# Four edits at the two ends of an attention and two-layer kernel: where the gate's exponential stands, zero products ahead of the first scores, the order of the first unit's row blocks, and a last evacuation in two halves

## The chip, the cores and the metric

The kernel runs on one core of a Trainium2 chip. The metric is device time in microseconds (us) of one launch. Three runs of the kernel before took 921.33, 922.25 and 922.31 us; the median is 922.25. A difference of 0.2% is 1.84 us.

## The reference

The reference is an attention layer with a memory path, followed by two gated feed-forward layers, all in float32.

```python
# attention: B, H, S, D = 4, 8, 576, 64
scores = (q @ k.T) / 8, masked above the diagonal
a = softmax(scores);  local = a @ v
q_p = phi(q)                      # phi(x) = (x if x > 0 else exp(x) - 1) + 1
mem_out = (q_p @ M_prev) / (q_p @ z_prev + 1e-6)
g = 1 / (1 + exp(-beta))          # one number per head, the gate
x = g * mem_out + (1 - g) * local # reshaped to 2304 tokens x 512
# layer 1: w_in 512 x 2048, w_out 2048 x 512
x = softplus(x @ w_in) @ w_out
# layer 2: w_a, w_b 512 x 1536, w_out 1536 x 512
out = ((x @ w_a) * (x @ w_b)) @ w_out
```

## The kernel before

The program is recorded as a list of steps, each with the tiles that it reads and writes. Afterwards `Plan.order` places the steps on the five engines with a model of its own: each step has a time and a lag (the time from its end until a reader may start), set in `weigh`. TensorE (PE) keeps the order in which its steps were recorded, first all of the attention, and of the later stages only what fits where the model sees it wait. On VectorE (DVE), ScalarE (ACT), GpSimd (POOL) and the DMA queue of SyncE (SP) the ready step with the longest chain behind it goes first, and a step that isn't ready in the model is passed by. So a change of one lag can reorder steps far away. The orders are fixed when the program is built; on the chip each engine takes its own list from the front and waits where an operand is missing.

**Attention.** There are 16 units, each of two heads of one batch. For a unit, `loads_k` and `loads_v` fetch the operands (tiles kr, qr, vr) and `prep_k` splits k and q into a high and a low part (kh, kl, qh, ql; line 343 is the subtraction), so that three products of fast float32 give full precision. `score` (line 517) forms row blocks of 128 queries: block 0 is 128 keys wide, block 1 256, block 2 384 and block 3 512, for two heads. DVE then takes each block's row minimum with the mask (line 527, tiles eTrue and eFalse, numbers in mn) and ACT its exponential (line 531). The last 64 queries of two units at a time are done by `tails` (line 668) and `score_tail` (line 538, tile eT). So units come in pairs: the tails stand with the even unit, after its successor's operands are there.

Per unit, `prep_v` and `prep_v2` form phi (ACT lines 498 and 499, DVE line 502, tiles ph and pos), `memory` multiplies it with M and z (line 555) and divides (tiles nm and mo). M has been multiplied by the gate: `gates` (lines 441 to 448) loads beta by a DMA of eight words per partition (tile bt, line 685), takes its exponential on ACT, and finishes on POOL and DVE; `load_m` (line 456) multiplies on POOL. `turn` (line 597, copies at 603 and 605) transposes the exponentials, `turn_tail` (lines 614 to 618) those of the tails, `send` (lines 570 to 576) passes the reciprocal row sums through DRAM by two stores, one of nine rows of 128 words and one of 64 words, and reads them back spread over the partitions (tile rb); `finish` (line 643) multiplies by them (tile xx) and stores. PSUM has eight banks. The scores take banks 2 and 3 (block 2), 0 and 1 (blocks 0 and 1) and 4 and 5 (block 3), the tails of a pair banks 0, 1 and 4, 5, and the transposes go round the same banks, so each of these waits for the engine that empties the bank before it.

While the attention runs, DVE, ACT and POOL also decode and split the first weights of layer 1 (lines 757 to 770, tiles raw and wf) in what time is left.

**Layers.** Each of the four products is done by seven products of half-size blocks in three passes (lines 875 and 1019). The last stage (`Wide.group`, line 1019) writes the output of a token group; the very last block is copied out of PSUM by one ACT instruction (line 1032) and stored by one DMA on SP's queue (line 1061).

Of the kernel before, what the change touches and what calls it, by code (L numbers as in the profile page):

```python
# [10 lines left out]
F32R = mybir.dt.float32r  # L11
U32 = mybir.dt.uint32
AF = mybir.ActivationFunctionType
# [9 lines left out]
HALF = 384  # L23
GT = 2 * HALF
NG = NT // GT
# [6 lines left out]
START, CONST, WORDS = 6272, 1280, 55680  # L32
SWITCH, LANES, AHEAD = 190, 6, 500
TAIL = 4
SEND, SENDC = 0, 5
RINGS = [2, 3, 0, 1, 4, 5], [4, 5, 2, 3, 0, 1]

# [18 lines left out]
class Plan:  # L56
# [103 lines left out]
    def weigh(self, s):  # L160

        kw, call = s.kw, s.call.__name__
        size = lambda ap: ap.free_size()
        o = kw["ap" if call == "memset" else "out"]
        inp = lambda ap: hasattr(ap, "tensor") and ap.tensor.name == self.psum
        s.size, s.mode, n = 0, None, size(o)
        two = call in ("tensor_tensor", "scalar_tensor_tensor", "tensor_tensor_reduce")
        s.port = s.eng == "POOL" or s.eng == "DVE" and not any(inp(v) for v in kw.values()) and n > 64
        if call == "dma_start":
            run = min(self.run(o), self.run(kw["in_"]))  # L170
            each = 14.5 + run / 4.85 if o.tensor.name in self.place else 33.3 + run / 8.7
            s.size = o.nbytes() / (4 * run) * each / 16
            s.time, s.lag = 420, 3000
        elif s.eng == "PE":
            s.lag = 205
            if call == "transpose" or kw.get("is_transpose"):
                s.time = n / 1.2 + 3
                s.mode = 128, 128, True
            else:
                plain = kw["rhs"].dtype != F32R  # L180
                rows, cols = (64 if x <= 64 else 128 for x in (kw["lhsT"].partition_size(), size(kw["lhsT"])))
                s.time = (1 + plain) * max(n / 1.2 + 3 if plain else n / 2.4 + 13.3, cols * 0.42 * (128 // rows))
                s.time /= 16384 / rows / cols
                s.mode = rows, cols, False, plain
        elif s.eng == "DVE":
            s.lag = 125
            s.time = n / (0.96 if two or any(inp(v) for v in kw.values()) else 1.92) + 68
            if hasattr(kw.get("scalar1"), "tensor"):
                s.time += 64
        elif s.eng == "ACT":  # L190
            s.lag = 50 if "accum_out" in kw else 145
            s.time = n * 0.834 + (50 if inp(kw["in_"]) else 94) + (184 if "accum_out" in kw else 0)
            if not isinstance(kw.get("scale", 1.0), float) or kw.get("scale") == REBIAS:
                s.time += 90
        else:
            s.lag = 90
            s.time = n * 2.1 + 210 if two else n * 0.82 + 200
# [126 lines left out]
def tile_kernel(ctx: ExitStack, tc: tile.TileContext, qt, kt, vt, mz, be, w_in, w_out, w_a, w_b, w_2, out):  # L324
    nc = tc.nc
    plan = Plan(tc)
    V, A, G, PE, SP = (
        Engine(plan, n, e) for n, e in (("DVE", nc.vector), ("ACT", nc.scalar), ("POOL", nc.gpsimd), ("PE", nc.tensor), ("SP", nc.sync))
    )

    def f(ap):
        return ap.bitcast(F32)
# [18 lines left out]
    bank = plan.track(nc.alloc_psum_tensor("bank", [128, 8, 512], F32).ap())  # L351
# [43 lines left out]
    RAW, WL, X0, X1, X2, SUMS = 0, 4096, 14848, 25600, 36352, 49664  # L395
# [3 lines left out]
    for n, words in (("kr", S), ("qr", 640), ("qh", 512), ("ql", 512), ("kh", S), ("kl", S), ("ph", 640)):  # L399
        at = [early(words), early(words)] + [more(words)] * (n in ("kr", "qr"))  # L400
# [23 lines left out]
        return bank[:, k : k + 2] if wide else bank[:, k]  # L424

    nc.scalar.preload_act_table_set("exp_and_others")
    G.memset(ap=ident, constant=0.0)
    G.affine_select(out=ident, in_=ident, compare_op=ALU.not_equal, fill=1.0, base=0, pattern=[[-1, 128]], channel_multiplier=1)
    G.memset(ap=mask1, constant=0.0)
# [2 lines left out]
    for j in range(2):  # L432
        G.affine_select(
            out=mask2[64 * j : 64 * j + 64, 1, 224:], in_=mask2[64 * j : 64 * j + 64, 1, 224:], compare_op=ALU.is_ge, fill=MASKED,
# [5 lines left out]
    def gates():  # L440
        A.activation(out=gt, in_=bt, func=AF.Exp, scale=-1.0)
        G.tensor_scalar(out=gt, in0=gt, scalar1=1.0, scalar2=1.0, op0=ALU.mult, op1=ALU.add)
        V.reciprocal(out=gt, in_=gt)
        pairs = gt.rearrange("p (n j) -> p n j", j=2)
        for odd in range(2):
            for j, r in enumerate(both):
                rnd(G, gp[r, odd::2], pairs[r, odd::2, j ^ odd])
        G.tensor_scalar(out=og, in0=gt, scalar1=-1.0, scalar2=1.0, op0=ALU.mult, op1=ALU.add)
# [4 lines left out]
    def load_m(b):  # L453
        m = mzs[b % 2]
        SP.dma_start(out=m, in_=mz[b])
        G.tensor_tensor(out=m[:, :, 0:64], in0=m[:, :, 0:64], in1=gp.unsqueeze(2).to_broadcast([128, NP, 64]), op=ALU.mult)
# [220 lines left out]
    def attention():  # L677
        nu = len(order)
        for name, part in (("eT", slice(S, 640)),):
            for t in where[name][0]:  # L680
                G.memset(ap=t[:, part], constant=0.0)
        for t in where["vr"][0]:
            G.memset(ap=t[low, 512:640], constant=0.0)
        order[0].loads_k()
        A.dma_start(out=bt, in_=be.partition_broadcast(128))
        order[1].loads_k()
        order[0].loads_v()
        order[0].prep_k(True)
        order[1].prep_k()
        order[0].prep_v()  # L690
        gates()
        load_m(0)
        at = lambda n: order[n] if 0 <= n < nu else None
        for n in range(nu + 2):
            cur, prev, old, nxt = (at(n - d) for d in (0, 1, 2, -1))
            if cur:
                if n % 2 == 0:
                    cur.begin()
                cur.score(2, 2)
                cur.score(0, 0, 1)  # L700
                cur.score(4, 3)
            if prev:
                prev.memory(2)
            if nxt and n:
                nxt.prep_k()
            if cur:
                cur.prep_v2()
            if n + 2 < nu:
                order[n + 2].loads_k()
            if cur and n:  # L710
                cur.loads_v()
            if nxt:
                if nxt.p == 0:
                    load_m(nxt.b)
                nxt.prep_v()
            if old:
                old.use()
                old.finish()
            if cur:
                if n % 2 == 0:  # L720
                    nxt.begin()
                    tails(((cur, 0), (nxt, TAIL)))
                cur.sums()
                cur.over()
            if prev:
                rings["psT"] = [RINGS[n % 2], 0]
                if n % 2:
                    prev.send(bank[0:10, SEND, 0:128])
                prev.turn(A, [(0, 0)])
                prev.turn(V, [(1, 0)])  # L730
                prev.turn(A, [(0, 1), (0, 3)])
                prev.turn(V, [(1, 1), (1, 3)])
                prev.turn(A, [(0, 2), (1, 2)])
                prev.turn_tail()
                prev.spread()
                if cur and n % 2:
                    cur.send(bank[0:10, SENDC, 0:128])

    attention()


# [214 lines left out]
    class Wide:  # L956
# [69 lines left out]
        def group(self, g):  # L1026


            def out(m):
                def out_(i, j, s, bank):  # L1030
                    if bank is not None:
                        A.activation(out=s, in_=bank, func=AF.Copy)
                    self.store(g, 2 * (2 - i) + m, j - 1, s)

                return out_

            units = [Seven(self.mult(m), out(m)) for m in range(2)]

            def piece(n, k):
                def go():  # L1040
                    if k == 0:
                        for u in units:
                            u.open(n)
                        if n in (5, 6, 7, 4):
                            self.sums(n)
                    x = self.parts(n, k)
                    for u in units:
                        u.mm(n, x, k)
                    if k == self.nu // 2 - 1:
                        for u in units:  # L1050
                            u.after(n)

                return go

            return [piece(n, k) for n in SEQ for k in range(self.nu // 2)]
# [1 line left out]
    def store_y(g, m, j, s):  # L1057
        SP.dma_start(out=ys[g][:, m, HALF * j : HALF * j + HALF], in_=s)

    def store_out(g, m, j, s):  # L1060
        SP.dma_start(out=out[128 * m : 128 * m + 128, GT * g + HALF * j : GT * g + HALF * j + HALF], in_=s)

    second = Wide(
        NU1, gs, wod,
# [177 lines left out]
```

## Time and profile before

| | |
|---|---|
| median of three runs | 922.25 us |
| span of the profiled execution, first to last instruction | 918.2 us |
| between the two | 4.05 us |
| PE busy | 905.9 us (99%) |
| DVE busy | 786.6 us (86%) |
| ACT busy | 564.9 us (62%) |
| POOL busy | 100.4 us (11%) |

The page gives the profiled execution by its span only; the 4.05 us stand for what lies around it. The chain that ended last runs over PE for 98% of the span. In a row of the timeline, the first two numbers are the start and the time from there to the end of the last of the merged instructions; the bracket at the end tells how long the engine had been idle and what ended that. PE's ends are modelled, so the distance of starts tells its pace better than a row's length.

### The profile page before, as it was taken

To read this page: it belongs to the slowest core of one execution; us is meant where nothing else is said; L and a number is where in the kernel's file an instruction comes from. 1 tells how busy PE (TensorE), PEld (TensorE's weight loads), DVE (VectorE), ACT (ScalarE), POOL (GpSimd) and SP (SyncE) were. 2 spreads that over 40 slices of the span, in tenths; PEclk is the share of its full clock that TensorE was granted. 3 is DMA by queue.
4 is the path that set the end of the run, shared out by engine and by line. 5 is a ranking of instruction groups with operands and counts; after the bars stand their busy time and mean duration, and the time that the engine had idled before them with its cause. 6 is when DMAs were issued, how large, how long until landed. Compare 5 with 4: busy or idle time off the path is not lost.

```text
span 918.2 us, 17626 instructions
## 1 busy us (share of the span) xinstructions
PE 905.9 (99%) x6556; PEld 868.2 (95%) x6556; DVE 786.6 (86%) x1487; ACT 564.9 (62%) x1124; POOL 100.4 (11%) x140
## 2 busy tenths in 40 slices
PE   6999999999999999999999999999999999999998
PEld 4777778899999999999999999999999999999998
DVE  6999999789999658988599999999899666988683
ACT  7999999677677576744456655444444344655442
POOL 6445667100000000000000000000000000000000
PEclk9999999999999999999999999999999999999999
DMA  7656654468889889672720445455656156672701
GB/s 231 192 157 184 191 155 127 135 237 273 287 305 303 290 296 374 218 246 80 225 75 23 161 149 181 161 167 179 215 185 220 48 185 186 227 248 88 215 26 52
DMA packets 84870, 172.16 MB, mean 187 GB/s; under 512 B 8352, under 2 KB 60976, under 8 KB 82096
## 3 DMA queue, kind: packets, MB, share of 16 engines
q1 hardware_dynamic: 84352, 170.71, 56.9%
q8 instruction: 51, 0.84, 0.4%
q10 hardware_dynamic: 432, 0.33, 0.1%
q14 instruction: 35, 0.29, 0.1%
HBM read 110.90 MB, written 60.11 MB: 186 GB/s over the span
## 4 chain that ended last, share of the span: by engine, by line
PE 98%; DVE 1%; DMA 0%; issue 0%; ACT 0%; SPq 0%; DVEq 0%
PE bank L875 48%; PE bank L1019 33%; PE bank L627 4%; PE bank L597 4%; PE bank L517 4%; PE bank L555 1%; PE bank L668 1%; PE bank L647 1%; PE bank L614 1%; PE bank L635 1%; DVE eTrue L527 0%; DMA kr<-kt 0%; PE bank L570 0%; PE bank L653 0%; PE bank L615 0%
## 5 line engine op out<-in xcount | busy, mean ns | idle before, releaser
L346 DVE TENSOR_TENSOR s<-bank,s 128x384 f32<-128x384 f32 x216 | 117.9, 552 | 40.8 <-PE bank L875 31.5
L853 ACT ACTIVATE s<-bank 128x384 f32<-128x384 f32 x72 | 35.0, 486 | 81.2 <-PE bank L875 52.0
L343 DVE TENSOR_TENSOR t<-t,t 128x1536 f32<-128x1536 f32 (+1 forms) x48 | 74.5, 1552 | 0.4
L875 PE MATMUL bank<-x1h,w 128*128 128x384 f32 x240 | 70.7, 335 | 0.0
L875 PE MATMUL bank<-x5h,w 128*128 128x384 f32 x240 | 70.6, 334 | 0.0
L875 PE MATMUL bank<-x3h,w 128*128 128x384 f32 x240 | 70.5, 334 | 0.0
L875 PE MATMUL bank<-x7h,w 128*128 128x384 f32 x240 | 70.5, 334 | 0.0
L875 PE MATMUL bank<-x6h,w 128*128 128x384 f32 x240 | 70.5, 334 | 0.0
L875 PE MATMUL bank<-x2h,w 128*128 128x384 f32 x240 | 70.5, 334 | 0.0
L875 PE MATMUL bank<-x4h,w 128*128 128x384 f32 x240 | 70.5, 334 | 0.0
L336 ACT ACTIVATE w<-wf 128x256 fp32r<-128x256 f32 (+1 forms) x100 | 50.1, 501 | 19.4 <-DVE w L343 14.7
L911 ACT ACTIVATE s<-s 128x384 f32<-128x384 f32 x72 | 37.5, 523 | 32.9 <-DVE s L346 32.5
L850 ACT ACTIVATE s<-bank 128x384 f32<-128x384 f32 x72 | 34.9, 485 | 32.1 <-PE bank L875 16.6
L336 ACT ACTIVATE gx1h<-t 128x768 fp32r<-128x768 f32 x37 | 31.3, 847 | 34.4 <-PE bank L1019 33.1
L336 ACT ACTIVATE gx2h<-t 128x768 fp32r<-128x768 f32 x37 | 31.4, 847 | 34.2 <-PE bank L1019 31.8
L343 DVE TENSOR_TENSOR w<-wf,w 128x256 fp32r<-128x256 f32 (+1 forms) x90 | 47.3, 525 | 3.7 <-ACT w L336 3.2
L336 ACT ACTIVATE gx0h<-t 128x768 fp32r<-128x768 f32 x37 | 31.3, 846 | 30.4 <-PE bank L1019 28.9
L759 ACT ACTIVATE raw<-raw 128x512 f32<-128x512 f32 (+1 forms) x54 | 43.2, 802 | 9.0 <-DVE raw L758 8.6
L343 DVE TENSOR_TENSOR gx1l<-t,gx1h 128x768 fp32r<-128x768 f32 x37 | 35.3, 954 | 13.5 <-ACT gx1h L336 13.3
L343 DVE TENSOR_TENSOR gx0l<-t,gx0h 128x768 fp32r<-128x768 f32 x37 | 35.3, 954 | 12.8 <-ACT gx0h L336 12.5
L856 ACT ACTIVATE s<-bank 128x384 f32<-128x384 f32 x72 | 35.3, 490 | 17.1 <-PE bank L875 12.9
L336 ACT ACTIVATE gx3h<-t 128x768 fp32r<-128x768 f32 x36 | 30.4, 845 | 24.1 <-PE bank L1019 24.0
(340 smaller groups left out, 2982.1 us busy)
## 6 DMA issues: line engine op xcount, KB each, us to landing
gs<-s SPq DMA_DIRECT2D x96, 192.0 KB
t<-gs SPq DMA_DIRECT2D x24, 768.0 KB
us<-s SPq DMA_DIRECT2D x72, 192.0 KB
t<-us SPq DMA_DIRECT2D x12, 768.0 KB
raw<-w_out SPq DMA_DIRECT2D x8, 1024.0 KB
raw<-w_in SPq DMA_DIRECT2D x12, 512.0 KB
raw<-w_a SPq DMA_DIRECT2D x12, 512.0 KB
raw<-w_b SPq DMA_DIRECT2D x12, 512.0 KB
```

The lines of the kernel that those rows point to most:

```text
L336: A.activation(out=o, in_=i, func=AF.Copy)
L343: eng.tensor_tensor(out=o, in0=a, in1=b, op=ALU.subtract)
L346: eng.tensor_tensor(out=o, in0=a, in1=b, op=ALU.add)
L517: PE.matmul(out=s[:, j, at : at + L], lhsT=a[r, qc], rhs=b[r, 0:L], start=t == 0, stop=t == 2, skip_group_check=True,)
L597: PE.transpose(out=s[:, 128 * n : 128 * n + 128], in_=Es[i, j][:, 128 * k : 128 * k + 128], identity=ident)
L627: PE.matmul(out=self.po[both[j], 128 * k :], lhsT=self.vr[:, k, 64 * j : 64 * j + 64], rhs=a, start=False, stop=k == 3, skip_group_check=True,
L759: A.activation(out=f(high), in_=f(high), func=AF.Identity, scale=REBIAS)
L853: A.activation(out=self.s5, in_=bank["c"], func=AF.Copy)
L856: A.activation(out=self.s2, in_=bank["b"], func=AF.Copy)
L875: PE.matmul(out=o, lhsT=w(n, a, k), rhs=x[n][c][:, k], start=start and k == t == 0, stop=k == 1 and t == 2, skip_group_check=True,)
L911: A.activation(out=s, in_=s if bank is None else bank, func=AF.Softplus)
L1019: PE.matmul(out=o, lhsT=self.w[n][a][:, u, 128 * m : 128 * m + 128], rhs=x[c][:, j], start=start and u == t == 0, stop=u == self.nu - 1 an ...
```

## The change

There are four edits.

1. In `weigh`, the lag of a DMA whose runs are at most 64 words goes from 3000 to 5500 ns in the model. This concerns the load of beta (8 words) and the 64-word store in `send`, of which there are 16. It adds no instruction, but moves many on DVE, ACT, POOL and SP. On ACT the gate's exponential, formerly right behind the first two qh, comes behind both phi steps, the first score exponential and the second unit's qh. On POOL the gate's steps come behind the second unit's kl and ql, and the multiplication of M behind the third unit's kh and kl.
2. A tile `idle` of 256 zero words is set by POOL first of all, and PE does 35 products of 128 x 128 with it into a bank that nothing reads, ahead of the first scores.
3. The first unit does blocks 0 and 1 before block 2. Its loads and splits come in the order that this asks for.
4. In the last group, the last block (m = 1, the one that comes from the bank) is copied in two halves of 192 columns and stored by two DMAs, the first on SP's queue, the second on ACT's.

```diff
-            s.time, s.lag = 420, 3000
+            s.time, s.lag = 420, 3000 if run > 64 else 5500
...
     nc.scalar.preload_act_table_set("exp_and_others")
+    idle = plan.buffer("idle", 256, X0, F32R)
+    G.memset(ap=f(idle), constant=0.0)
+    for _ in range(WAKE):
+        PE.matmul(out=bank[:, 7, 0:128], lhsT=idle[:, 0:128], rhs=idle[:, 128:256], start=True, stop=True, skip_group_check=True)
...
-                cur.score(2, 2)
+                if n:
+                    cur.score(2, 2)
                 cur.score(0, 0, 1)
+                if not n:
+                    cur.score(2, 2)
                 cur.score(4, 3)
...
+                    if bank is not None and m and g == NG - 1 and self.store is store_out:
+                        h = HALF // 2
+                        for part, q in ((slice(0, h), SP), (slice(h, HALF), A)):
+                            A.activation(out=s[:, part], in_=bank[:, part], func=AF.Copy)
+                            self.store(g, 2 * (2 - i) + m, j - 1, s, part, q)
+                        return
```

WAKE is 35. Three places show what moves. In the rows of an order stand the line, the operation and its tiles, written ones first; the lines of the changed kernel are higher by 5 in the attention's functions.

PE, the head of its list, before:

```order
L517 MATMUL bank<-kh_74,qh_70 128x384 x2
L517 MATMUL bank<-kl_76,qh_70 128x384 x2
L517 MATMUL bank<-kh_74,ql_72 128x384 x2
L517 MATMUL bank<-kh_74,qh_70 128x128 x2
L517 MATMUL bank<-kl_76,qh_70 128x128 x2
L517 MATMUL bank<-kh_74,ql_72 128x128 x2
```

The same place in the changed kernel:

```order
L431 MATMUL bank<-idle 128x128 x35
L522 MATMUL bank<-kh_74,qh_70 128x128 x2
L522 MATMUL bank<-kl_76,qh_70 128x128 x2
L522 MATMUL bank<-kh_74,ql_72 128x128 x2
L522 MATMUL bank<-kh_74,qh_70 128x256 x2
L522 MATMUL bank<-kl_76,qh_70 128x256 x2
L522 MATMUL bank<-kh_74,ql_72 128x256 x2
L522 MATMUL bank<-kh_74,qh_70 128x384 x2
```

The zeros stand ahead, and block 2 (384 wide) comes behind blocks 0 and 1. Otherwise PE's list differs in one place: near the end of the attention, four products of layer 1 (tile x5) move up from behind the last unit's products to ahead of its transposes.

DVE, behind the first unit's row minima, before (gt is the gate, ph is phi, eT are the tails of units 0 and 1):

```order
L443 RECIPROCAL gt_59<-gt_59 128x8
L502 SCALAR_TENSOR_TENSOR ph_78<-ph_78,pos_80 128x640
L538 ISA eT_97,mn_127<-bank,mask_57 128x576
L538 ISA mn_127 128x1
L538 ISA eT_98,mn_128<-bank,mask_57 128x576
L538 ISA mn_128 128x1
L527 ISA eTrue_85,mn_128<-bank,mask_56 128x384
```

In the changed kernel the phi of unit 0 stands behind all eight row minima of unit 1, whose last three open these rows:

```order
L532 ISA eTrue_88,mn_128<-bank,mask_56 128x512
L532 ISA mn_128 128x1
L532 ISA eFalse_96,mn_128<-bank,mask_56 128x256
L532 ISA mn_128 128x1
L532 ISA eFalse_94,mn_128<-bank,mask_56 128x128
L532 ISA mn_128 128x1
L507 SCALAR_TENSOR_TENSOR ph_78<-ph_78,pos_80 128x640
L592 RECIPROCAL rs_133<-ss_131 128x10
L564 SCALAR_TENSOR_TENSOR nm_129<-bank,rs_133 128x10
L565 RECIPROCAL nm_129<-nm_129 128x10
L576 COPY rt_107<-bank 9x128
L566 TENSOR_TENSOR mo_103<-bank,nm_129 128x2x5x64
```

So the memory products of unit 0, which read ph, come later than the second unit's minima, and the division (nm, mo) right behind them.

DVE, ahead of the tails of units 6 and 7, before:

```order
L561 TENSOR_TENSOR mo_104<-bank,nm_130 128x2x5x64
L761 SCALAR_TENSOR_TENSOR wf<-raw_62 128x2x256
L643 TENSOR_TENSOR xx_123<-bank,rb_121 128x512
L654 TENSOR_TENSOR xx_123<-bank,rb_121 128x64
L538 ISA eT_97,mn_127<-bank,mask_57 128x576
L538 ISA mn_127 128x1
```

The same place in the changed kernel:

```order
L566 TENSOR_TENSOR mo_104<-bank,nm_130 128x2x5x64
L507 SCALAR_TENSOR_TENSOR ph_78<-ph_78,pos_80 128x640
L765 TENSOR_SCALAR raw_63<-raw_63 128x512 x2
L766 SCALAR_TENSOR_TENSOR raw_63<-raw_63 128x512
L543 ISA eT_97,mn_127<-bank,mask_57 128x576
L543 ISA mn_127 128x1
L543 ISA eT_98,mn_128<-bank,mask_57 128x576
L543 ISA mn_128 128x1
L648 TENSOR_TENSOR xx_123<-bank,rb_121 128x512
L659 TENSOR_TENSOR xx_123<-bank,rb_121 128x64
```

The two xx, which need the sums that went through DRAM, have gone behind the tails, and phi and steps of the weight decoding stand ahead of them.

## Rows read from the trace of the kernel before

**Rows 1.** The page: the span, and the chain by engine.

```profile
span 918.2 us, 17626 instructions
...
PE 98%; DVE 1%; DMA 0%; issue 0%; ACT 0%; SPq 0%; DVEq 0%
```

**Rows 2.** Waits of PE, longest first: us in total, times, longest.

```profile
PE bank L517 <- DVE kh L338: 5.1, 1, 5.1
...
PE bank L517 <- ACT aT L603: 0.6, 1, 0.6
```

**Rows 3.** Windows: length, PE, PEld, DVE, ACT, POOL busy, granted clock, DMA share, GB/s.

```profile
0.00:10.00 10.00, 4.23 (x24) 3.03 (x24) 4.50 (x17) 5.42 (x12) 6.90 (x21) 1.00 0.76 233
...
30.00:40.00 10.00, 9.97 (x139) 7.89 (x138) 9.98 (x34) 10.00 (x29) 4.19 (x7) 1.00 0.71 220
```

**Rows 4.** Timeline of PE: scores of unit 0, tails, scores of unit 1.

```profile
8.26 0.63 PE L517 MATMUL bank<-kl,qh 64*128 64x512 f32 x2
8.68 0.63 PE L517 MATMUL bank<-kh,ql 64*128 64x512 f32 x2
10.92 1.50 PE L668 MATMUL bank<-kr,qr 64*64 64x288 f32 x16 [1.61 <-DVE mn L527]
...
14.20 0.39 PE L517 MATMUL bank<-kl,qh 64*128 64x512 f32 x2
...
14.43 0.39 PE L517 MATMUL bank<-kh,ql 64*128 64x512 f32 x2
```

**Rows 5.** Timeline of DVE: row minima of unit 0, phi, tails, memory's division.

```profile
6.90 0.56 DVE L527 CUSTOM_DVE_ANT_0 eTrue<-bank,mask 128x384 f32<-128x384 f32 x1 [0.56 <-PE bank L517]
...
7.38 0.55 DVE L527 CUSTOM_DVE_ANT_0 eTrue<-bank,mask 128x384 f32<-128x384 f32 x1
...
9.35 0.69 DVE L527 CUSTOM_DVE_ANT_0 eTrue<-bank,mask 128x512 f32<-128x512 f32 x1 [0.50 <-PE bank L517]
...
10.79 0.29 DVE L527 CUSTOM_DVE_ANT_0 eFalse<-bank,mask 128x128 f32<-128x128 f32 x1
...
11.11 0.77 DVE L502 SCALAR_TENSOR_TENSOR ph<-ph,pos 128x640 f32<-128x640 f32 x1
12.35 0.76 DVE L538 CUSTOM_DVE_ANT_0 eT<-bank,mask 128x576 f32<-128x576 f32 x1 [0.47 <-PE bank L668]
...
17.05 0.80 DVE L561 TENSOR_TENSOR mo<-bank,nm 128x640 f32<-128x640 f32 x1
```

**Rows 6.** Timeline of ACT: the gate's exponential; unit 0's last transpose copy.

```profile
6.70 0.21 ACT L441 ACTIVATE gt<-bt 128x8 f32<-128x8 f32 x1 [1.43 <-DMA bt<-be]
...
22.52 0.67 ACT L603 ACTIVATE aT<-bank,og 128x512 f32<-128x512 f32 x1
```

**Rows 7.** Timeline: the tails of units 2 and 3.

```profile
29.24 0.42 DVE L757 TENSOR_SCALAR raw<-raw 128x512 uint32<-128x512 uint32 x1
...
29.57 0.75 DVE L538 CUSTOM_DVE_ANT_0 eT<-bank,mask 128x576 f32<-128x576 f32 x1
...
30.38 0.33 PE L597 MATMUL bank<-ident,eFalse 128*128 128x128 f32 x1
```

**Rows 8.** Timeline: the tails of units 6 and 7.

```profile
67.73 0.68 DVE L761 SCALAR_TENSOR_TENSOR wf<-raw 128x512 uint32<-128x512 uint32 x1
...
68.33 0.68 DVE L643 TENSOR_TENSOR xx<-bank,rb 128x512 f32<-128x512 f32 x1
...
69.34 0.76 DVE L538 CUSTOM_DVE_ANT_0 eT<-bank,mask 128x576 f32<-128x576 f32 x1 [0.20 <-PE bank L668]
...
70.17 0.32 PE L597 MATMUL bank<-ident,eFalse 128*128 128x128 f32 x1
```

**Rows 9.** Timeline: the last copy and the last store.

```profile
914.95 0.49 ACT L1032 ACTIVATE s<-bank 128x384 f32<-128x384 f32 x1 [0.55 <-PE bank L1019]
915.47 0.33 SPq L1061 DMA_DIRECT2D out<-s  x1
```

**Rows 10.** A window in the last store's transfer.

```profile
916.40:916.80 0.40, 0.00 (x0) 0.00 (x0) 0.00 (x0) 0.00 (x0) 0.00 (x0) 1.00 1.00 369
```

More of the change, by code (lines that the diff above doesn't have):

```diff
@@ L34 @@
 TAIL = 4
+WAKE = 35
 SEND, SENDC = 0, 5
@@ L1058, in store_y, with store_out @@
         SP.dma_start(out=ys[g][:, m, HALF * j : HALF * j + HALF], in_=s)
-    def store_out(g, m, j, s):
-        SP.dma_start(out=out[128 * m : 128 * m + 128, GT * g + HALF * j : GT * g + HALF * j + HALF], in_=s)
+    def store_out(g, m, j, s, part=slice(0, HALF), q=SP):
+        at = GT * g + HALF * j
+        q.dma_start(out=out[128 * m : 128 * m + 128, at + part.start : at + part.stop], in_=s[:, part])
     second = Wide(
```

## The prediction

> **What bounds the kernel now.** I read the page first. The span is 918.2 us and 98% of the chain that ended last runs over PE [rows 1]. So an edit is worth what it takes from PE's idle time or from PE's slow stretches, and it costs what it puts there. PE's own waits come next: the longest is the 5.1 us for the first operands, and no wait later than 30 us is in that list, one of its last being for ACT's copy of unit 0 [rows 2]. Then the windows. In the first 10 us PE has 4.23 us of work, but from 30 us on PE, DVE and ACT are all at 9.97 to 10.00 of 10 [rows 3]: there the three engines run level, and work that comes late on DVE or ACT shows on PE at once. What can be gained lies therefore ahead of 30.38 us, where PE has its last short wait [rows 7], and behind the last product, where the copy starts at 914.95 [rows 9].
>
> All sums are made in the profiled execution's 918.2 us. The median of the runs shown is 922.25, 4.05 more; I take these 4.05 as unchanged and subtract the gain from the median. What a measurement of this kernel can tell from no change is about 0.2%, 1.84 us: faster means below 920.41, slower above 924.09.
>
> **The zero products.** In the scores of unit 0 two products of 512 columns start 0.42 us after the two before (8.26, 8.68); in unit 1 the same pair takes 0.23 (14.20, 14.43) [rows 4]. So PE ran at the lower of its two levels (1.2 GHz against 2.4) up to 9.1 us, though the granted clock reads 1.00 in that window as everywhere [rows 3]. It rose somewhere between there and the tails at 10.92, that is 4.0 to 5.8 us after its first product at 5.08. A zero product of 128 columns takes 0.107 at the lower level (a quarter of 0.42), 35 of them 3.7 us. They start at about 1.1 (an estimate: POOL sets 256 words first) and lie in the 5.1 us wait [rows 2]. If the rise follows the first product by the same time, it comes at 5.1 to 6.9. The bound below: if each zero product pays for its weight load as well, 0.21 each, they last until 8.6 and hold up the first scores; the row for 64-row products gives no hint of that, and I take 0.107.
>
> **Small blocks first.** DVE's preparation ended at 6.34 (6.90 less its 0.56 idle) [rows 5]. It is the same six instructions in another order, so about 6.5. A row minimum holds DVE for 0.48 at 384 columns (6.90 to 7.38); a row overlaps the next by 0.08, so 512 take 0.61, 128 take 0.21, and 256, between them, about 0.35 [rows 5]. All eight are 3.30; before they took from 6.90 to 11.00, since DVE waited for slow products (0.50 at 9.35 alone) [rows 5]. Now the order is 256, 256, 128, 128, 384, 512, 512, 384, and the tails need the banks of the first seven: 6.5 + 0.70 + 0.42 + 0.48 + 1.22 = 9.3 instead of 10.92. If PE were still at the lower level, block 3 would come 0.75 later. So PE is 1.6 us ahead at the tails.
>
> **Phi goes behind unit 1's minima.** Those 1.6 us are given back. Before, phi of unit 0 took 0.77 at 11.11 in a gap in which DVE had to wait for the tails anyway [rows 5]; it cost nothing. Now: tails' minima from 10.8 (9.3 and the 1.43 between 10.92 and 12.35), 2 x 0.68, the gate 0.1, eight minima 3.30, phi 0.70: 16.2. PE has finished unit 1's scores before 13 and has nothing else in its list: it is idle for some 3.3 us until phi is there. The memory products and the division follow, and mo starts at about 17.6 (an estimate, 17.1 if the products cost nothing, 18.0 with 1 us for them) against 17.05 [rows 5]. The transposes that wait for its banks are then 0.5 later than before, not earlier. The gate's POOL work, which now stands behind kh and kl of unit 2, ends ahead of phi by the sum of its steps, so phi hides it; without that cover it would cost what it is late.
>
> **The gate's exponential.** ACT sat idle 1.43 us for beta [rows 6]. Now phi goes ahead, and ACT waits only for the first row minimum, about 0.35 at 6.6. So ACT is 1.05 ahead, and since its list is full from there on, it is still 1.05 ahead at 22.52, at the copy for which PE's third unit waited [rows 2, 6]. This is the lead that survives: PE's block 3 of unit 2 starts 1.05 earlier, for phi has by then been paid for.
>
> **To 30 us.** The phi inputs of unit 1 end on ACT where that copy starts, 21.5. From there DVE does a decoding step (0.33, from 29.24 to 29.57 [rows 7]), phi 0.70, eight minima 3.30, the division's two small steps 0.2, mo 0.72, phi 0.70, a decoding step 0.33 and one of 0.60 (67.73 to 68.33 [rows 8]): 28.4, where the tails' minima of units 2 and 3 start; before, 29.57 [rows 7]. PE's third group of transposes, 30.38 before, moves by the same 1.15. PE itself would be there at 28.7, so it waits about 0.5 for DVE. I take 1.1 for the whole start, with bounds of -2.3 (zero products at double price) and 1.7 (PE alone limits).
>
> **The longer lag, later.** The model now thinks that the sums through DRAM land 2.5 us later. So at the pair 6 and 7 the two xx have gone behind the tails, and phi and decoding have come in. Before, 1.61 us lay between mo and the tails' minimum, with 0.20 of them idle [rows 8]; now 0.70 + 2 x 0.33 + 0.60 = 1.96. PE started its third group 0.83 after that minimum started, 0.68 of them being the minimum [rows 8], so it has hardly any slack: 0.35 us lost. The pairs 4 and 5, and 8 and 9, get the same 1.96 and had 1.88 and 1.76 (sums of the same prices for what stood there): 0.1 and 0.2. In the last three pairs less stands there than before. Sum 0.65; as DVE may arrive a little earlier elsewhere, I take 0.6, with bounds 0 and 3.8 (0.94 of decoding at each of four pairs). The other moves, in layer 1's preparation and of its four products, change no amount of PE's work; I cost them at nothing, hidden by PE's full list, and at what they are late if that list runs dry.
>
> **The last evacuation.** One copy takes 0.49 and its store is issued from 915.47 to 915.80 [rows 9]. Two half copies end between 915.44 and 915.93 (a half at half or at full price); I take 915.6, and the second issue's end 915.95, 0.15 late. The transfer moved at 369 GB/s with all engines busy [rows 10], so 192 KB take 0.53 and half of it 0.27. The end moves by 0.15 - 0.27: 0.1 gained, bounds -0.3 and 0.3.
>
> **Sum.** 1.1 - 0.6 + 0.1 = 0.6 us: a span of 917.6, and 922.25 - 0.6 = 921.65, said as 921.6.
>
> **Rivals.**
>
> DVE keeps up. The decoding steps cost PE nothing, since DVE has lost its waits too and reaches each pair earlier. Then PE alone limits the start (1.7), and the tail gives its 0.2: 920.35. For it: DVE's idle time before 11 us shrinks by more than PE's. Against it: 9.98 of 10 in the windows from 30 us [rows 3].
>
> The clock falls again. The new idle stretch of 3.3 us between unit 1's scores and phi has no equal in the trace, whose longest idle time after the first product is the 1.61 ahead of the tails, and the products behind it were not slow [rows 4]. If PE comes back at the lower level, all that it does from phi to DVE's next copies takes twice as long, as in rows 4: memory products and two groups of transposes, some 1.65 us at the upper level (an estimate, 0.8 and 0.85). The start then loses 1.65 of its 1.1, and the time is 923.3. The Trainium skill, "TensorE: Matmul & The Clock Gate" (section "Why this matters for your kernels"), says that gaps of idle PE between bursts in mid-kernel put it back to the lower clock; it speaks against moving phi. By that rule the sum would be this rival's, by the trace's 1.61 us it stays as it is.
>
> Slower: the decoding ahead of the tails. If each of the four pairs from units 2 and 3 on pays the whole 0.94 of decoding on PE, as the first does for half, and the odd units, whose transposes wait for mo, a like amount once, that is 4.7 us against 1.2 gained: 925.75. It becomes slower by 0.2% once the waits pass 3.05 us. For it: level load of three engines [rows 3] and third groups that follow DVE at once [rows 7, 8]. Against it: the same kind of steps stood there before, and PE has no wait after 30.38.
>
> The zero products hold up the scores at 0.21 each: 925.
>
> The zeros do not lift the clock in time: block 3 is 0.75 later, but ACT's lead decides, so 921.9; I count it with the forecast.
>
> **Chances.** Forecast 0.43, DVE keeps up 0.34, clock falls 0.10, decoding slower 0.09, zeros hold up 0.04. Of the second, two thirds lie below 920.41, of the forecast a tenth: faster 0.26. The last two make slower 0.13. Same: 0.61. The range takes in the forecast with 0.8 to each side, most of the second case and the third: 919.8 to 923.4.
>
> **What would show it.** Zero products from about 1.1 to 4.9, and pairs of 512 columns 0.23 apart in unit 0. The tails' products near 9.3. Phi of unit 0 on DVE near 15.5, PE idle for about 3 us before it, mo near 17.6. The copy of 22.52 near 21.5. The tails' minimum of units 2 and 3 near 28.4, with PE waiting for it; waits of 0.1 to 0.35 at the next three pairs and none later. The last store landing 0.1 earlier. I am wrong if PE waits in the odd units, if the second half's store lands last by more than 0.3, or if the lead at 30 us is not kept to 170.

## The result: slower by half a per cent, and the profile after

The changed kernel took 926.39 us (median of 5, 925.88 to 926.56), the kernel before beside it 921.33 (921.02 to 922.31): a ratio of 1.0051, with an interval of 1.0039 to 1.0063. 921.6 was predicted from a median of 922.25, with a range up to 923.4: a gain of 0.6 us was forecast, and 5.1 were lost. The answer is that the 35 zero products cost twice what the sum gave them, did not raise the clock in unit 0's scores, and held these up by 3.7 us.

The page of the changed kernel, and PE's waits (us in total, times, longest), beside [rows 1, 2]:

```profile
span 924.0 us, 17720 instructions
...
PE 96%; DVE 2%; issue 1%; DMA 1%; ACT 0%; POOL 0%; SPq 0%; DVEq 0%; ACTq 0%; POOLq 0%
```

```profile
PE bank L560 <- issue: 3.3, 1, 3.3
PE bank L431 <- POOL idle L429: 1.1, 1, 1.1
```

The wait of 5.1 us for the first operands is gone, since PE was busy with zeros. A single wait of 3.3 us ahead of the memory products is new. PE's timeline, in the columns of [rows 4]:

```profile
1.10 7.73 PE L431 MATMUL bank<-idle 128*128 128x128 f32 x35 [1.10 <-POOL idle L429]
8.76 0.47 PE L522 MATMUL bank<-kh,qh 64*128 64x128 f32 x2
...
11.60 0.63 PE L522 MATMUL bank<-kl,qh 64*128 64x512 f32 x2
12.02 0.63 PE L522 MATMUL bank<-kh,ql 64*128 64x512 f32 x2
12.58 2.65 PE L673 MATMUL bank<-kr,qr 64*64 64x288 f32 x16
...
16.77 0.40 PE L522 MATMUL bank<-kl,qh 64*128 64x512 f32 x2
17.01 0.39 PE L522 MATMUL bank<-kh,ql 64*128 64x512 f32 x2
20.69 1.36 PE L560 MATMUL bank<-mz,ph 64*64 64x65 f32 x40 [3.29 <-issue]
```

35 products in 7.73 us are 0.221 each. The first scores start at 8.76 instead of 5.08, and the pairs of 512 columns in unit 0 are still 0.42 apart (11.60, 12.02), as in [rows 4], 10.5 us after PE's first zero. In unit 1 they are 0.24 apart. Then PE is idle from 17.40 to 20.69, and the forty memory products behind it take 1.36. DVE, in the columns of [rows 5]:

```profile
10.56 0.42 DVE L532 CUSTOM_DVE_ANT_0 eFalse<-bank,mask 128x256 f32<-128x256 f32 x1 [4.72 <-PE bank L522]
...
14.93 0.76 DVE L543 CUSTOM_DVE_ANT_0 eT<-bank,mask 128x576 f32<-128x576 f32 x1 [0.45 <-PE bank L673]
...
19.77 0.82 DVE L507 SCALAR_TENSOR_TENSOR ph<-ph,pos 128x640 f32<-128x640 f32 x1
...
22.61 0.80 DVE L566 TENSOR_TENSOR mo<-bank,nm 128x640 f32<-128x640 f32 x1
```

DVE had finished its preparation at 5.83 and waited 4.72 us for the scores that stood behind the zeros. ACT waited as long (first row below), so the gate's exponential, which now stands later in ACT's list, saved it nothing; the copy that came at 22.52 in [rows 6] comes at 26.57:

```profile
11.03 0.51 ACT L536 ACTIVATE eFalse<-eFalse,mn 128x256 f32<-128x256 f32 x1 [4.80 <-DVE mn L532]
...
12.06 0.19 ACT L446 ACTIVATE gt<-bt 128x8 f32<-128x8 f32 x1
...
26.57 0.69 ACT L608 ACTIVATE aT<-bank,og 128x512 f32<-128x512 f32 x1
```

The windows, in the columns of [rows 3] (the seventh number is the granted clock):

```profile
0.00:10.00 10.00, 8.90 (x47) 8.79 (x49) 2.04 (x6) 3.37 (x5) 5.60 (x19) 1.00 0.75 226
...
30.00:40.00 10.00, 10.00 (x151) 7.80 (x149) 9.96 (x34) 9.92 (x30) 3.26 (x5) 1.00 0.74 236
```

```profile
20.50:21.00 0.50, 0.31 (x12) 0.34 (x16) 0.22 (x2) 0.50 (x3) 0.32 (x2) 0.50 0.92 344
...
23.00:23.50 0.50, 0.50 (x5) 0.50 (x4) 0.41 (x1) 0.50 (x3) 0.42 (x2) 0.50 0.00 1
23.50:24.00 0.50, 0.50 (x6) 0.50 (x5) 0.03 (x1) 0.23 (x1) 0.50 (x1) 1.00 0.05 9
```

When PE comes back behind its idle 3.29 us, the granted clock is 0.50 (1.2 of 2.4 GHz), and it stays there up to 23.5. The Trainium skill, "TensorE: Matmul & The Clock Gate" (section "Why this matters for your kernels"), says that idle gaps put PE back to the lower clock; here the trace agrees. From 30 us on the three engines run level again, as in [rows 3]. PE's transposes at the tails of units 2 and 3 and of units 6 and 7, beside [rows 7, 8], and the end, beside [rows 9, 10]:

```profile
34.59 0.33 PE L602 MATMUL bank<-ident,eFalse 128*128 128x128 f32 x1
...
75.18 0.33 PE L602 MATMUL bank<-ident,eFalse 128*128 128x128 f32 x1
```

```profile
920.90 0.55 ACT L1042 ACTIVATE s<-bank 128x192 f32<-128x192 f32 x2 [0.55 <-PE bank L1027]
921.25 0.33 SPq L1076 DMA_DIRECT2D out<-s  x1
921.48 0.35 ACTq L1076 DMA_DIRECT2D out<-s  x1
```

PE's third group of transposes starts at 34.59 instead of 30.38: 4.2 us late. At 75.18 (70.17 before) it is 5.0, at the end 5.8. So most of the loss, 4.2 of 5.8, is there at the tails of units 2 and 3. From the first copy of the last block to the end of the span 3.1 us pass, 3.25 before.

### The profile page after: what moved, and what is told of

Read it like the earlier page. It is cut to its first block, busy times and chain, and to the rows that moved or that the text cites. A ratio compares the mean times of both kernels' runs of the same rounds, so it can differ in the third digit from the quotient of the medians.

```text
span 924.0 us, 17720 instructions
## 1 busy us (share of the span) xinstructions
PE 915.3 (99%) x6591; PEld 876.9 (95%) x6591; DVE 787.8 (85%) x1487; ACT 564.8 (61%) x1125; POOL 100.2 (11%) x141
## 4 chain that ended last, share of the span: by engine, by line
PE 96%; DVE 2%; issue 1%; DMA 1%; ACT 0%; POOL 0%; SPq 0%; DVEq 0%; ACTq 0%; POOLq 0%
PE bank L883 47%; PE bank L1027 32%; PE bank L632 4%; PE bank L602 4%; PE bank L522 3%; PE bank L560 1%; PE bank L673 1%; PE bank L652 1%; PE bank L431 1%; PE bank L640 1%; PE bank L619 1%; DMA qr<-qt 0%; DVE t L344 0%; DVE w7l L344 0%; PE bank L575 0%
## 5 line engine op out<-in xcount | busy, mean ns | idle before, releaser
L344 DVE TENSOR_TENSOR gx0l<-t,gx0h 128x768 fp32r<-128x768 f32 x37 | 35.4, 956 | 15.5 <-ACT gx0h L337 15.2
```

The lines of the kernel that those rows point to most:

```text
L344: eng.tensor_tensor(out=o, in0=a, in1=b, op=ALU.subtract)
```

## The experiments

Each ran in five rounds beside the kernel before, if nothing else is said; e14 and e15 in three, e16 once. The kernel before had medians of 921.08 to 921.45 in them.

**Theory** after the result: the zero products hold up the scores, and this is nearly the whole loss. **Rivals**: phi behind unit 1's minima, with the clock that falls ahead of it; the longer lag.

In the code below, `...` and the lines left out stand for what is as in the change; where a kernel's products are wider, its tile `idle` is longer too.

**e1_no_zeros, e2_no_blocks, e3_zeros_only, e4_no_lag: one part out, or one part alone.** e1 drops the zeros from the changed kernel, e2 the order of the blocks, e4 the lag; e3 adds the zeros to the kernel before.

```diff
 e1
-    for _ in range(WAKE):
-        PE.matmul(out=bank[:, 7, 0:128], lhsT=idle[:, 0:128], rhs=idle[:, 128:256], ...)
 e2
-                if n:
-                    cur.score(2, 2)
+                cur.score(2, 2)
                 cur.score(0, 0, 1)
-                if not n:
-                    cur.score(2, 2)
 e4
-            s.time, s.lag = 420, 3000 if run > 64 else 5500
+            s.time, s.lag = 420, 3000
```

> The changed kernel without its 35 zero products. Theory (the zero products hold up the scores, 0.22 us each until 8.76): the first scores start at about 5.1 again, the first row minimum at about 6.9 instead of 10.56, phi of unit 0 near 16.1 instead of 19.77, the tails of units 2 and 3 near 28.9 instead of 32.60, and all of the 3.7 us comes off: about 922.7. Rival (the moved phi and the moved decoding are the cause, PE's later waits swallow the zeros): less than 1 us comes off, 925.4 or more.

Measured: 922.21 (ratio to before 1.0011, 1.0002 to 1.0020), 4.2 less than the changed kernel: near the theory's 922.7 and far from the rival. PE's wait ahead of the memory products (3.63 us) is still there, so it is not what the 4.2 us were.

> The changed kernel with the first unit's blocks in the old order (block 2, 0 and 1, 3). Phi of unit 0 then stands ahead of the tails on DVE again. Theory (the held-up scores cost most, phi behind unit 1's minima costs little): PE's idle 3.3 us ahead of the memory products goes, and with it the stretch at granted clock 0.5, but the tails come at 14.6 instead of 12.58; about 925. Rival (the moved phi is the main cause, with the clock that falls behind it): 923 or less.

Measured: 924.22 (1.0036, 1.0023 to 1.0048), between the two. So with the zeros in place the order of the blocks costs 2.2 us; with the 4.2 of e1 that is more than the whole loss, so the parts don't add up. PE's idle 3.3 us and the low stretch are gone, but M times the gate is late:

```profile
19.25 0.81 PE L560 MATMUL bank<-mz,ph 64*64 64x65 f32 x40 [1.32 <-POOL mz L461]
```

> The kernel before with the 35 zero products alone. Theory: first scores at 8.8 instead of 5.08, the tails of units 2 and 3 at 31.6 instead of 28.20; the whole 3.4 to 3.7 us shows at the end: 924.7 to 925.0 beside 921.3. Rival (PE's own waits of 3.1 us between 10 and 25 us swallow the delay): under 922.5.

Measured: 925.31 (1.0046, 1.0034 to 1.0059): 4.0 us for the zeros alone. The later waits swallow nothing. There is a wait on top that the kernel before does not have:

```profile
127.48 0.32 PE L522 MATMUL bank<-kh,qh 64*128 64x128 f32 x1 [0.50 <-DVE aT L622]
```

All six kernels that add products to the kernel before without the lag (e3, e9, e14 to e17) have it, with 0.50 to 0.55 us, whatever the products' shape.

> The changed kernel with all lags at 3000, so that the gate's exponential and the decoding stand where they stood. Theory: the distance to the kernel before still grows by 1.5 us from the tails of units 2 and 3 (4.4) to the end (5.9) in the changed kernel, and this growth is the lag's: 924.9 here. Rival (that growth comes from the late start itself): 926.4, as the changed kernel.

Measured: 927.57 (1.0071, 1.0058 to 1.0083). Both were wrong: in this company the lag gains 1.2. Without it phi took 1.41 us beside POOL's work, and PE was idle for 3.95 us ahead of the memory products, which came at 21.17. The growth that the theory gave to the lag is there without it: PE's tails of units 2 and 3 start 5.67 us later than before (33.80), those of the last pair 7.37 (154.91).

**e12_after_wide, e14_zeros_256, e15_narrow_16, e16_narrow_ones: the price of the products and the clock.** e12 has the changed kernel's zeros in another shape; the other three are the kernel before with products of one kind added.

```diff
 e12
-    for _ in range(WAKE):
-        PE.matmul(out=bank[:, 7, 0:128], lhsT=idle[:, 0:128], rhs=idle[:, 128:256], ...)
+    for _ in range(8):
+        PE.matmul(out=bank[:, 7, 0:512], lhsT=idle[:, 0:128], rhs=idle[:, 128:640], ...)
 e14
+    for _ in range(17):
+        PE.matmul(out=bank[:, 7, 0:256], lhsT=idle[:, 0:128], rhs=idle[:, 128:384], ...)
 e15: as the change, with range(16)
 e16: as the change, with
+    G.memset(ap=f(idle), constant=1.0)
```

> The changed kernel with its 35 zero products of 128 columns replaced by eight of 512. Theory (only the price of the products was wrong, and phi still comes late): the first scores at about 5.1, unit 0's pairs 0.23 apart, phi near 16, PE idle for over 3 us ahead of it and a low granted clock behind it: 922 to 922.5, as without zero products. Rival (the lifted clock is worth something by itself): 921 or less.

Measured: 921.87 (1.0007, 0.9998 to 1.0016). The one loop in another shape gives back 4.5 of the 5.1 us. PE's timeline and two windows:

```profile
1.42 3.78 PE L431 MATMUL bank<-idle 128*128 128x512 f32 x8 [1.42 <-POOL idle L429]
5.13 0.33 PE L522 MATMUL bank<-kh,qh 64*128 64x128 f32 x2
...
6.68 0.40 PE L522 MATMUL bank<-kl,qh 64*128 64x512 f32 x2
6.91 0.40 PE L522 MATMUL bank<-kh,ql 64*128 64x512 f32 x2
...
16.28 1.36 PE L560 MATMUL bank<-mz,ph 64*64 64x65 f32 x40 [3.29 <-POOL ss L587]
```

```profile
16.00:18.00 2.00, 1.72 (x43) 1.63 (x44) 0.66 (x4) 2.00 (x9) 1.84 (x4) 0.50 0.49 184
...
20.00:22.00 2.00, 2.00 (x11) 2.00 (x10) 1.13 (x2) 0.69 (x1) 1.35 (x3) 0.50 0.95 212
```

This is the start that the prediction meant: scores at 5.13 at the upper level, pairs 0.23 apart, PE idle 3.29 us until phi. But the granted clock is 0.50 in the windows from 16 to 22, and what the early scores gained is gone again.

> The kernel before with 17 zero products of 256 columns (4352 columns). Theory (a product takes the longer of its columns and a floor of 0.21 us): 0.21 each, done near 4.9, nothing held up, 921.2. Rival (weight load and columns add up, 0.107 + 0.213): 0.32 each, done near 6.7, the first scores 1.6 us late and 922.5 or more. Open is whether the clock is up when unit 0's scores start.

Measured: 920.87 (0.9997, 0.9988 to 1.0006).

```profile
1.20 3.99 PE L430 MATMUL bank<-idle 128*128 128x256 f32 x17 [1.20 <-POOL idle L428]
...
7.12 0.40 PE L521 MATMUL bank<-kl,qh 64*128 64x512 f32 x2
7.36 0.39 PE L521 MATMUL bank<-kh,ql 64*128 64x512 f32 x2
```

3.99 us for 17 are 0.23 each: 256 columns take what 128 take, so load and columns do not add up. Unit 0's pairs of 512 columns run at the upper level.

> The kernel before with 16 zero products of 128 columns. At 0.22 each they are done at 4.7, ahead of the first scores at 5.08: 921.2, and the clock still low in unit 0 (pairs of 512 columns 0.43 apart), if narrow products don't raise it. Rival (a burst costs by itself, by its buffer or its clock): 922 or more.

Measured: 921.87 (1.0012, 1.0003 to 1.0021): almost free (0.4 by the medians; its wait of the kind shown under e3 is 0.52), and nothing raised.

```profile
1.10 3.67 PE L430 MATMUL bank<-idle 128*128 128x128 f32 x16 [1.10 <-POOL idle L428]
4.95 0.69 PE L521 MATMUL bank<-kh,qh 64*128 64x384 f32 x2 [0.18 <-DVE kh L338]
...
8.12 0.63 PE L521 MATMUL bank<-kl,qh 64*128 64x512 f32 x2
8.55 0.63 PE L521 MATMUL bank<-kh,ql 64*128 64x512 f32 x2
```

> As e3_zeros_only, with ones in place of zeros. Theory (width decides): the same 0.22 each until 8.8, unit 0's pairs of 512 columns still 0.43 apart, the clock up only behind 11 us. Rival (zeros are why they didn't count): pairs 0.23 apart from the first score on, and products of less than 0.22 behind some 5 us.

Measured: 925.41 (one run), 35 products in 7.73 us and unit 0's pairs 0.43 apart. So ones do as little as zeros.

**e10_rsd_only, e11_gate_only, e5_lag_halves, e13_halves_only: the lag and the halves without the rest**, all on the kernel before.

```diff
 e10
+            s.time, s.lag = 420, 5500 if run == 64 else 3000
 e11
+            s.time, s.lag = 420, 3000 if run > 8 else 5500
 e5: the change's lag, and the halves;  e13: the halves
```

> The kernel before with the gate's lag and the last evacuation in halves alone (no zero products, old order of the blocks). Theory: the longer lag gains, since all lags at 3000 made the changed kernel 1.2 us slower (927.57 against 926.39), and the halves gain 0.1: 920.1 beside 921.3. Rival (that 1.2 us was the start with phi at 19.66 that took 1.41 us, and not the lag): no difference, 921 to 922.

Measured: 922.95 (1.0022, 1.0013 to 1.0031). Both wrong: the lag loses here (e13 has the halves without it).

> The kernel before with the longer lag for the load of beta alone, so that the gate's exponential goes behind phi and POOL's gate steps come late. Theory: M times the gate starts at about 16.3 instead of 13.72, the memory products at about 17 instead of 14.75, and the time is 922.5 to 922.9. Rival (ACT's lead of 1.05 us is what survives, as predicted): 920 to 920.5.

Measured: 922.39 (1.0010, 1.0001 to 1.0018), 1.2 lost, at the place that the theory named (POOL, then PE):

```profile
15.48 0.61 POOL L456 TENSOR_TENSOR mz<-mz,gp 128x256 f32<-128x256 f32 x1
```

```profile
16.15 1.28 PE L555 MATMUL bank<-mz,ph 64*64 64x65 f32 x40 [1.34 <-POOL mz L456]
```

With phi in its old place, PE waits 1.34 us for M times the gate, whose exponential ACT has put behind other work. Behind that wait the granted clock is 0.50 from 16.5 to 19.5, so the loss holds a slow stretch too.

> The kernel before with the longer lag for the 64-word stores and reads of the reciprocal row sums alone (the gate stays where it was, and so does all up to the third unit). Theory (the 1.8 us that lag and halves cost in e5_lag_halves come from the late gate): 921.1 to 921.7, of which up to 0.6 for decoding steps ahead of the tails. Rival (the reshuffle of decoding and xx costs it): 922.5 or more, with PE waiting for DVE between 40 and 100 us.

Measured: 924.27 (1.0031, 1.0019 to 1.0042), 3.1 lost: the rival's size, and its place for a part. PE's products of the tails stood level with before at 28.07 (28.13), 0.8 late at 68.91 (68.11) and 1.4 late at 148.95 (147.54). PE waits for DVE at 42.31 (0.26) and at 65.17 (0.15), which it does not before. The next loss is a wait of layer 1:

```profile
170.19 0.44 PE L875 MATMUL bank<-x1h,w 128*128 128x384 f32 x1 [0.50 <-ACT aT L603]
```

The rest of the 3.1, about a third, was not traced.

> The kernel before with the last evacuation in two halves on two queues alone. Theory (0.1 us gained at the end, as predicted): 921.1, no difference that the times can show; in the trace the last transfer ends 0.1 to 0.3 us earlier behind the last product. Rival (the second half's store on ACT's queue lands late, and part of the 1.8 us of e5_lag_halves is the halves'): 921.7 or more.

Measured: 920.86 (0.9997, 0.9988 to 1.0007). No cost, and from the first half's copy to the span's end again 3.1 us. (Of the traces with halves, those of e6 and e7 have 3.45 there, more than the 3.25 of before.)

**e6_phi_first and e7_nozero_phi: phi by hand.** In the changed kernel (e7: without zeros) phi of unit 0 gets the first rank on DVE; the lines that add `first` to the rank are left out.

```diff
             V.scalar_tensor_tensor(out=self.ph, in0=self.ph, scalar=1.0, in1=self.pos, ...)
+            if self.b == self.p == 0:
+                plan.steps[-1].first, plan.steps[-1].port = FIRST_PHI, False
```

> The changed kernel, zero products and small blocks included, with phi of unit 0 put by hand behind the first row minimum. Theory (what the small blocks cost is that they send phi behind unit 1's minima): the memory products start at about 18.5, when M times the gate is there, instead of 20.69, no stretch at granted clock 0.5 behind them, and 2.2 to 2.5 us come off the 926.4: about 924. Rival (the blocks cost through the gate's later steps on POOL, which stay late): less than 0.8 comes off, 925.6 or more.

Measured: 924.79 (1.0044, 1.0031 to 1.0057). Of the right sign, but not for the reason given: phi stood ahead of minima for which the tails waited, and PE's clock stayed low up to the memory products, which came at 20.50 and not at 18.5. Inconclusive for phi.

> As e6_phi_first and without the zero products. Theory: both losses gone, the memory products at about 16.7, the tails of units 2 and 3 near 28.2, and 920.0 to 920.5, under the 921.3 of the kernel before. Rival (with phi early the small blocks still gain nothing, since M times the gate comes at 16.6 against 14.3 before): 921.3 or more.

Measured: 923.52 (1.0026, 1.0015 to 1.0037), 1.3 worse than e1. The start is as expected (tails of units 2 and 3 at 28.55), but from the 25th step on ACT's list is that of e10 up to the last block, and PE waits in the same place, 0.49 at 170.32. An edit to one rank thus moved the planner to another order, whose cost shows 140 us later.

**e8_wide_zeros, e9_wide_only, e17_zeros_halves: is there a better version?** e8 is e5 with the eight products of 512 columns, e9 the kernel before with them, e17 is e14 with the halves (no new lines).

> e5_lag_halves with eight zero products of 512 columns (4096 columns in all, where 35 of 128 columns are 4480). Theory (a product of 128 columns pays for its weight load as well as for its columns): eight times 0.43, done at 4.6 to 5.0, so they hold up nothing. Whether they lift the clock is open: if they do, unit 0's pairs of 512 columns start 0.23 apart instead of 0.43, the tails come up to 1 us earlier and the time is 919.5; if zeros as such don't count, the pairs stay at 0.43 and the time is that of e5_lag_halves.

Measured: 921.18 (1.0000, 0.9991 to 1.0009), 1.8 less than e5; unit 0's pairs are 0.24 apart. The 919.5 that was expected with the raised clock did not come: PE waits 1.83 us for M times the gate, and the granted clock is 0.50 from 15.5 to 18.5.

> The kernel before with eight zero products of 512 columns alone. Theory (they lift the clock ahead of the scores, as in e8_wide_zeros, and hold up nothing; the gate stays early): scores of unit 0 done near 7.8 instead of 9.26, the tails near 9.8 instead of 10.92, phi of unit 0 near 9.9 and the memory products near 13.7 instead of 14.75; that 1.1 us is kept: 920.0 beside 921.1. Rival (DVE's row minima and ACT's copies set the pace before 25 us, so PE's gain is swallowed): 920.8 to 921.4.

Measured: 921.45 (1.0004, 0.9995 to 1.0013). The memory products came at 13.79, as expected, but PE's transposes then waited for DVE:

```profile
16.95 0.33 PE L601 MATMUL bank<-ident,eFalse 128*128 128x128 f32 x1 [0.27 <-DVE mo L565]
20.61 0.27 PE L574 MATMUL bank<-ident,rs 128*10 128x128 f32 x1 [1.15 <-DVE rs L591]
```

Of 1.0 us ahead, 0.4 was left at the tails of units 2 and 3 (27.75 for 28.13), and none at 127.93 (127.55), behind the wait at 122.60 (0.55) that e3 has too.

> The two parts that cost nothing together: the kernel before with 17 zero products of 256 columns and the last evacuation in halves. Theory (PE's lead of 1 us at the memory products is taken back by DVE and ACT before 30 us, the halves give 0.1 to 0.2): 920.5 to 920.9, hardly to be told from the kernel before. Rival (the early rise of the clock spares every execution the slow stretch that some of the kernel before have): 919.5 or less.

Measured: 920.94 (0.9998, 0.9989 to 1.0007). In its profiled execution, the longest of 11, the granted clock was at 0.50 twice (11 to 13 and 25 to 27), after waits of 1.77 and 1.21 us, so an early rise does not spare an execution the slow stretches. No version was found that beats the kernel before.

## Why the prediction was wrong

- **The zero products: the step that failed.** "A zero product of 128 columns takes 0.107 at the lower level (a quarter of 0.42)": it took 0.221. The quarter scales with the columns, but below 256 columns the time no longer falls: 128 columns take what 256 take (e14). The trace of before had this price, a few rows above those of [rows 4], in unit 0's pairs at the lower level, and farther on, at the upper level, in its transposes, which are products of 128 x 128 too:

```profile
6.65 0.42 PE L517 MATMUL bank<-kl,qh 64*128 64x128 f32 x2
6.87 0.41 PE L517 MATMUL bank<-kh,ql 64*128 64x128 f32 x2
...
7.40 0.41 PE L517 MATMUL bank<-kl,qh 64*128 64x256 f32 x2
7.62 0.41 PE L517 MATMUL bank<-kh,ql 64*128 64x256 f32 x2
...
18.51 0.93 PE L597 MATMUL bank<-ident,eTrue 128*128 128x128 f32 x7
19.28 0.60 PE L614 MATMUL bank<-ident,eT 128*128 128x128 f32 x4
```

  Pairs of 128 columns start 0.22 apart there, as those of 256 do. The prediction said that the row for 64-row products gave no hint. Seven transposes of 128 x 128 take 0.77 us (18.51 to 19.28), 0.11 each at the upper level, where the columns' quarter of 0.23 would be 0.06: twice the columns' price here too. The prediction had the price as a bound ("until 8.6", measured 8.76) and as a rival (925, measured 926.39), at a chance of 0.04. By e3 and e12 this one term, with the later wait of 0.5 us in e3 and the raised clock in e12, is 4.0 to 4.5 of the 5.1 us. The Trainium skill, "TensorE: Matmul & The Clock Gate" (section "Back-to-back issue gap"), says that in a stream of loads and products both set the spacing; the trace agrees in so far as 0.221 is more than the columns' share, and the load is likely the floor, but no run here took it away.
- **The rise of the clock** "at 5.1 to 6.9" failed as well: in the changed kernel it came behind the pairs at 12.02, and 16 products of 128 columns (e15) or 35 with ones (e16) did not bring it either. With products of 256 or 512 columns (e8, e9, e12, e14, e17) unit 0's scores came to the upper level between 5.1 and 7.0, about where the prediction had it.
- **Small blocks and phi: right.** In e12, where the price is mended, phi came at 15.36 (predicted 15.5 to 16.2) and PE was idle for 3.29 us (predicted 3.3). The rival "the clock falls again", at 0.10, then came true on top: granted clock 0.50, and 1.36 us for memory products that took 0.81 in e14. The 1.61 us of idle time from which it was argued down was less than half as long, and is no safe evidence either: in e3 the same wait of 1.61 us is followed by a granted clock of 0.50 from 16 to 19. What the order of the blocks is worth depends on its company: 0.7 gained without zeros (922.21 in e1, 922.95 in e5), 0.7 lost with wide ones (921.87 in e12, 921.18 in e8), 2.2 lost with the narrow ones (926.39, and 924.22 in e2); of these only the last is clear of the noise.
- **"This is the lead that survives": wrong.** ACT's 1.05 us by the later gate were counted as a gain, and POOL, which takes the gate's result, as hidden by phi. Where phi was early, PE waited 1.3 us for M times the gate (e2, e11), and the lag for beta alone lost 1.2. "Phi hides it" held only as long as phi itself was late.
- **The longer lag, later: not settled.** 0.6 was predicted, within bounds up to 3.8. Alone, the lag for the 64-word stores cost 3.1 in the median (e10); there the sum had counted DVE's steps ahead of the tails, but not ACT's copies ahead of layer 1, where 0.50 were lost. In the changed kernel the distance to before grew from 4.40 at the tails of units 2 and 3 (32.53 against 28.13) to 5.46 (153.00 against 147.54). But without the lag it grew by more (e4), so this growth is not shown to be the lag's.
- **The last evacuation: right.** 0.1 predicted, 0.15 measured (3.25 to 3.1, in the changed kernel and in e13), in one trace each and too little for the medians to show.
- **The base.** The 4.05 us between span and median were not all what lies around an execution. In the runs whose spans are known, the time is some 1.8 us above the span (926.39 and 924.6 in the changed kernel's median run). So the profiled execution of before, with 918.2 us of span, took some 920.0 (an estimate), and was some 2.2 us shorter than the median run of 922.25. The distances of 4.2 to 5.8 us above are measured from this short execution. e13, with the same lists up to the last block, ended at 920.1; its clock rose later:

```profile
10.79 2.50 PE L669 MATMUL bank<-kr,qr 64*64 64x288 f32 x16 [1.61 <-DVE mn L528]
...
15.62 0.63 PE L518 MATMUL bank<-kh,qh 64*128 64x512 f32 x2
16.05 0.61 PE L518 MATMUL bank<-kl,qh 64*128 64x512 f32 x2
16.47 0.42 PE L518 MATMUL bank<-kh,ql 64*128 64x512 f32 x2
```

The tails take 2.50 here and 1.50 in [rows 4]. So a difference of under 2 us between the starts of two traces can be one between two executions; what a part costs is read from medians here.

## What to carry to other kernels

Price a filler product by the distance of starts in rows of products of its own shape, at the clock that holds where it stands, and end the filler well inside the wait, since what is behind it on an in-order engine pays for every mistake. When an edit moves a step off a busy engine, follow its result through each engine that handles it before counting a lead. Where a planner sets the order, an edit at the start can change lists far behind it, so undo each part alone before a loss is put down to the part that looks guilty, and do not expect the parts to add up.

## What was not expected of the hardware

- At the lower level a product of 128 columns with its own weight load took 0.221 us, and one of 256 columns hardly more (0.23, e14). At the upper level the transposes of before, of 128 columns, took 0.11.
- 7.73 us of products of 128 columns, zeros or ones, left unit 0's scores at the lower level; 3.78 us of 512 columns (e12) and 3.99 us of 256 (e14), all zeros, were followed by the upper one. So zeros count; why the narrow ones did not is not settled by these runs.
- Before and e13 have the same work on PE up to 17 us, but the level rose ahead of 10.92 in the one and near 16.3 in the other.
- Waits of PE much shorter than 3.29 us were followed by a granted clock of 0.50 too: 1.34 us in e11, 1.61 in e3, 1.83 in e8. The 1.61 of before was not.
